# Attention with two mixture-of-experts layers on one core: other first loads, a row pass of one width, and VectorE work given to GpSimd

## The chip, the cores and the metric

The kernel runs on one core of a Trainium2 chip. The metric is the device time of one execution in microseconds. Before the change it is 1004.54 us, the median of three runs (1000.55 to 1005.47).

## What is computed

Block-causal attention feeds a top-2 mixture of experts, and that feeds a top-1 mixture of experts.

```
q, k, v: (4, 8, 576, 64)                     # batch, heads, sequence, head size
scores = q @ k.T / 8; masked where block_i < block_j (blocks of 64)
x = softmax(scores) @ v  ->  (2304, 512)     # heads side by side
logits = x @ w_gate + log1p(exp(x @ w_noise)) * noise      # 8 experts
for each row: the two best experts, softmax over the two
x = sum of weight * (relu(x @ w1[e]) @ w2[e])              # w1 512x1024, w2 1024x512
logits = x @ w_gate2 + modality_bias[modality]
out = softmax weight of the best expert * (relu(x @ m2w1[e]) @ m2w2[e])
```

All products are fp32 in quality: most are made of three products of high and low parts (`kh`/`kl`, `wh`/`wl`, `PTh`/`PTl`).

## The kernel before

The work runs in this order: 16 pairs of heads (4 batches of 4 pairs) in the attention, with the routing of finished batches beside it; then the experts of the first layer; then those of the second.

**A pair of heads** (`pair`, from L875) is cut into named steps. TK, TQ and T4 transpose k, q and their tails. KH, QH, A4 on ScalarE and KL, QL, D4 on VectorE make high and low parts. S0 to S8 are the scores, M the row maxima (`nm`, VectorE), E the exponentials (`p`, ScalarE, with row sums into `ss`). B transposes the exponentials, H and L split them into `PTh` and `PTl`. VX, V0, V1 are the products with v (`pa`), CX, C0, C1 copy them to `oT`.

**The row pass** (`xr`, L1074) is X0 and X1: for each head of the pair five products with `IW` (64 columns that turn `oT` into rows, and 16 columns of the gates) bring rows of 64 outputs and 16 gate logits into PSUM; four chunks have 128 rows, the last has 64 (L1078). XC0 and XC1 copy them to `xu`.

**R and R2** finish the softmax sums: GpSimd adds (R), VectorE takes four reciprocals of slices of `ss`, straight into `rr` (L1002, L1003). `out_rows` (L1090) multiplies `xu` by `rr` on GpSimd, into the rows `x` that are written to X1 in DRAM, and into `LH`, which holds the gate logits of all eight heads apart.

**Routing** (`route`, L650) runs three times, for batches 0 and 1 (behind pair 7), 2 (behind pair 11) and 3 (behind pair 15). It sums `LH` over heads by a reduction to `lg` (L659), picks the two best experts, counts places with products of `m`, and makes lists of rows per expert: `hot_b` (`sl_ob`) and `hot_a` (`sl_oa`, `sl_ov`) are one-hot arrays on VectorE, and `lists` multiplies them on TensorE, ten products for each batch. `early` (L1122) then turns part of the lists into indices (`si_u`, `ids`, `gp`, `idg`) and gathers the first rows of expert 0 and expert 1 from X1 into `wide` (`gather0`, L776).

**The first expert job** is planned with the attention (`first_steps`, L1162): JT, JH, JL bring its rows in, JM0 to JM7 are the eight hidden blocks (12 products each, `ps<-kh,wh`), JR and JV split them (`kp`), JS splits the next weights (`wl`). Its second matmul (`py`) and all later jobs follow in `run` (L1392), which transposes the gathered rows of the next job (`px`) between the halves of a second matmul.

**What sets the order.** TensorE, ScalarE and VectorE run what the loop from L1332 writes down: each step has a due time from a table (`SCHED`), the costs of L80 to L99 advance a clock for each engine, and the step that can start first, or is due first, is written next. GpSimd and SP get their instructions in the order in which that loop reaches them. An engine runs its list in order, so one late step holds what is written behind it.

**The start** (L1105 to L1113): nine matmuls on constant `ones`, then all loads of pair 0 to 2 on SP's queue, k and q of pair 0 first, then their tails, then v.

Of the kernel before, what the change touches and what calls it, by code (L numbers as in the profile page):

```python
# [30 lines left out]
def moe_kernel(tc, q, k, v, w_gate, w_noise, noise, w1, w2, mod_id, w_gate2, mod_bias, m2w1, m2w2, out):  # L31
# [72 lines left out]
    with ExitStack() as top:  # L104
# [9 lines left out]
        nc.scalar.preload_act_table_set("natural_log_exp_and_others")  # L114
# [167 lines left out]
        def hot_a(pool, a, n, a0, na, vals):  # L282

            oa = pool.tile([128, n, na], BF16, name="sl_oa")
            ov = pool.tile([128, n, NV, na], BF16, name="sl_ov")
            vec.tensor_tensor(oa, bc(lane[:, None, a0:a0 + na], [128, n, na]), bc(a[:, :, None], [128, n, na]), op=OP.is_equal)
            yield .8
            m = -(-n // 2) if n * na > 200 else n
            for c in range(0, n, m):
                s = slice(c, min(c + m, n))  # L290
                vec.tensor_tensor(ov[:, s], bc(oa[:, s, None, :], [128, s.stop - c, NV, na]),
                                  bc(vals[:, s, :, None], [128, s.stop - c, NV, na]), op=OP.mult)
                yield .3
            return ov
# [355 lines left out]
        def route(b0, nb):  # L650
# [6 lines left out]
            for b in range(b0, b0 + nb):  # L657
                c0 = 5 * (b - b0)
                vec.tensor_reduce(l[:, c0:c0 + 5], LH[:, b].rearrange("p c h e -> p c e h"), axis=AX, op=OP.add)  # L659
                yield .9  # L660
# [109 lines left out]
        LH = wide1[:, E * DM - B * 5 * H * 2 * E:].rearrange("p (b c h e) -> p b c h e", b=B, c=5, h=H)  # L770
# [33 lines left out]
        with ExitStack() as ph:  # L804
# [44 lines left out]
            def load(p, names):  # L849
# [7 lines left out]
                else:  # L857
                    r["t"] = ld.tile([128, 2, D], F32, name="tld")
                    tails = [(r["t"][64 * i:64 * i + 64], n) for i, n in enumerate("qk")]
# [3 lines left out]
                def ends():  # L863
                    for t, n in tails:
                        nc.sync.dma_start(t, src[n][b, 2 * hp:2 * hp + 2, 512:576, :].rearrange("h p d -> p h d"))
                if p:
                    ends()
                for n in names:
                    for i in range(2):
                        nc.sync.dma_start(r[n][:, 0:4, i, :],  # L870
# [4 lines left out]
            def pair(p):  # L875
# [214 lines left out]
                def out_rows():  # L1090
# [3 lines left out]
                    gps.tensor_tensor(LH[:, b, :, 2 * hp:2 * hp + 2].rearrange("p c h e -> p h c e"), xu[:, :, :, D:], rb(2 * E), op=OP.mult)  # L1094
# [11 lines left out]
            pw = ps_s.tile([128, 4, 128], F32, name="ps")  # L1106
            for _ in range(9):
                nc.tensor.matmul(pw, ones, bc(ones[:, None, :], [128, 4, 128]), start=True, stop=True)
            load(0, "kq")
            load(0, "v")  # L1110
            load(1, "kq")
# [155 lines left out]
            arrive = dict(zip(("TK", "TQ", "T4"), (4.2, 5.7, 6.8)))  # L1267
# [33 lines left out]
            def earliest(e, p, n):  # L1301
                t = clk[e] if p > 2 or n not in arrive else max(clk[e], arrive[n] + 5.5 * p)
# [390 lines left out]
```

## Time and profile before

| | |
|---|---|
| median of three runs | 1004.54 us (1000.55 to 1005.47) |
| profiled execution | 1002.42 us, span 1000.6 us |
| busy in the span: PE, DVE, ACT, POOL | 955.4, 723.9, 518.6, 492.9 us |
| chain that ended last | PE 72%, DVE 13%, issue 5%, ACT 3%, POOL 3%, DMA 2% |
| granted clock of TensorE, mean | 0.992 |

PE is TensorE's matmuls and PEld its weight loads, DVE is VectorE, ACT ScalarE, POOL GpSimd, SP SyncE. Nearly all instructions are recorded by one helper and so carry line L71: they are told apart by the tiles they write and read, as `ps<-kh,kp`. An fp32 matmul of the program is two weight loads and two matmuls in the trace. A row with "idle before" tells how long its engine stood idle and what ended that.

### The profile page before, as it was taken

To read this page: it belongs to the slowest core of one execution; us is meant where nothing else is said; L and a number is where in the kernel's file an instruction comes from. 1 tells how busy PE (TensorE), PEld (TensorE's weight loads), DVE (VectorE), ACT (ScalarE), POOL (GpSimd) and SP (SyncE) were. 2 spreads that over 40 slices of the span, in tenths; PEclk is the share of its full clock that TensorE was granted. 3 is DMA by queue.
4 is the path that set the end of the run, shared out by engine and by line. 5 is a ranking of instruction groups with operands and counts; after the bars stand their busy time and mean duration, and the time that the engine had idled before them with its cause. 6 is when DMAs were issued, how large, how long until landed. Compare 5 with 4: busy or idle time off the path is not lost.

```text
span 1000.6 us, 17459 instructions
## 1 busy us (share of the span) xinstructions
PE 955.4 (95%) x6058; PEld 863.6 (86%) x6058; DVE 723.9 (72%) x1761; ACT 518.6 (52%) x1156; POOL 492.9 (49%) x400
## 2 busy tenths in 40 slices
PE   7999998898999999999999999999999989999995
PEld 5988898787888997989899898989979879999994
DVE  5878879999968985568493957759788876455450
ACT  5989887778653253333333343333325445555551
POOL 6133141432221589768594857747476254333321
PEclk8999999999999999999999999999999999999998
DMA  5557743331067556555472745534366867776620
GB/s 126 103 156 229 208 122 82 77 82 50 26 202 254 95 138 187 131 138 115 107 147 75 161 105 127 123 80 64 110 149 178 288 215 241 225 223 216 209 84 13
DMA packets 158257, 141.59 MB, mean 142 GB/s; under 512 B 76233, under 2 KB 124745, under 8 KB 158034
## 3 DMA queue, kind: packets, MB, share of 16 engines
q1 hardware_dynamic: 140098, 107.18, 36.4%
q0 software_dynamic: 18064, 33.23, 16.5%
q8 instruction: 50, 0.82, 0.3%
q14 instruction: 45, 0.37, 0.1%
HBM read 112.54 MB, written 28.36 MB: 141 GB/s over the span
## 4 chain that ended last, share of the span: by engine, by line
PE 72%; DVE 13%; issue 5%; ACT 3%; POOL 3%; DMA 2%; SPq 1%; POOLq 0%; ACTq 0%
PE ph L71 28%; PE py L71 26%; PE pt L71 7%; PE ps L71 5%; PE pa L71 3%; PE px L71 2%; DVE nm L71 2%; DVE PTl L71 2%; DVE wl L71 2%; POOL wl L71 2%; ACT p L71 1%; DVE kp L71 1%; DMA xr<-X,ids 1%; ACT wh L71 1%; POOL LG L71 1%
## 5 line engine op out<-in xcount | busy, mean ns | idle before, releaser
L71 POOL TENSOR_TENSOR wl<-raw,wh 128x1024 fp32r<-128x1024 f32 x80 | 207.8, 2628 | 107.7 <-ACT wh L71 93.5
L71 PE MATMUL ph<-xth,wh 128*128 128x320 f32 (+2 forms) x800 | 240.9, 301 | 2.1 <-DVE kp L71 2.1
L71 PE MATMUL ph<-xth,wl 128*128 128x320 f32 (+2 forms) x800 | 239.7, 300 | 0.0
L71 PE MATMUL ph<-xtl,wh 128*128 128x320 f32 (+2 forms) x800 | 239.7, 300 | 0.0
L71 DVE SCALAR_TENSOR_TENSOR zero<-py,gts,wide 128x512 f32<-128x512 f32 x304 | 227.4, 748 | 8.3
L71 PE MATMUL py<-wh,kp 128*128 128x512 f32 x496 | 166.8, 396 | 0.0
L71 PEld LDWEIGHTS ph<-xth,wh 128*128 128x128 f32 x800 | 151.6, 189 | 3.7 <-DVE kp L71 2.9
L71 ACT ACTIVATE wh<-raw 128x1024 fp32r<-128x1024 f32 x144 | 150.9, 1053 | 2.8 <-DMA raw<-in_moe_w_dram 2.8
L71 PEld LDWEIGHTS ph<-xtl,wh 128*128 128x128 f32 x800 | 151.6, 190 | 0.7
L71 PEld LDWEIGHTS ph<-xth,wl 128*128 128x128 f32 x800 | 151.6, 189 | 0.0
L71 ACT ACTIVATE yr<-py,gts 128x512 f32<-128x512 f32 x60 | 41.4, 690 | 144.9 <-PE py L71 96.8
L71 PEld LDWEIGHTS py<-wh,kp 128*128 128x128 f32 x496 | 93.2, 188 | 18.3
L71 DVE SCALAR_TENSOR_TENSOR hl<-ph,hh 128x320 fp32r<-128x320 f32 (+2 forms) x100 | 46.3, 465 | 79.2 <-ACT hh L71 79.0
L71 PE MATMUL ps<-kh,kp 128*128 128x256 f32 (+5 forms) x320 | 98.4, 349 | 3.5 <-ACT p L71 1.5
L71 DVE TENSOR_TENSOR wl<-raw,wh 128x1024 fp32r<-128x1024 f32 x64 | 79.7, 1253 | 29.6 <-ACT wh L71 29.5
L71 PE MATMUL py<-wl,kp 128*128 128x512 f32 x248 | 96.7, 390 | 0.0
L71 POOL DMA_INDIRECT xr<-X,ids x55 | 58.7, 1066 | 72.9 <-PE px L71 44.2
L71 PE MATMUL py<-wh,hh 128*128 128x512 f32 x232 | 93.9, 405 | 0.0
L71 PE MATMUL py<-wl,hh 128*128 128x512 f32 x232 | 90.5, 390 | 1.7 <-POOL wl L71 1.7
L71 PE MATMUL py<-wh,hl 128*128 128x512 f32 x232 | 90.7, 391 | 0.0
L71 ACT ACTIVATE hh<-ph 128x320 fp32r<-128x320 f32 (+2 forms) x100 | 41.9, 418 | 93.6 <-PE ph L71 90.4
L71 DVE TENSOR_TENSOR xtl<-px,xth 128x512 fp32r<-128x512 f32 x58 | 40.0, 689 | 68.1 <-ACT xth L71 68.0
(249 smaller groups left out, 1822.0 us busy)
## 6 DMA issues: line engine op xcount, KB each, us to landing
raw<-in_moe_w_dram SPq DMA_DIRECT2D x144, 512.0 KB, 4.0
X<-zero SPq DMA_DIRECT2D x13, 512.0 KB, 4.3
kld<-in_k_dram SPq DMA_DIRECT2D x32, 128.0 KB, 2.8
qld<-in_q_dram SPq DMA_DIRECT2D x32, 128.0 KB, 2.9
vld<-in_v_dram SPq DMA_DIRECT2D x32, 128.0 KB, 2.7
X<-x SPq DMA_DIRECT2D x16, 256.0 KB, 2.4
wide<-in_moe_w_dram SPq DMA_DIRECT2D x4, 512.0 KB, 4.7
wide<-WG2T POOLq DMA_DIRECT2D x1, 2048.0 KB, 11.6
```

The costliest lines, as they stand in the source:

```text
L71: return f(*a, **kw)
```

## The change

It has seven parts.

- The loads of q of pair 0 are issued on ScalarE's queue, ahead of the loading of the activation table; on SP's queue k and q of pair 1 go ahead of v of pair 0.
- `spin` writes matmuls on `ones` wherever the loop sees a gap of more than 0.6 us on TensorE's clock in the first 60 us: 23 in all against 9.
- The last chunk of the row pass takes 128 columns of `oT` (rows 448 to 575); the copy takes the upper half.
- R2 is one reciprocal on VectorE (`ri`) and four copies on GpSimd that place it in `rr`.
- `LH` holds two sums: the first pair of a batch writes it, the others multiply in place and add, on GpSimd; the reduction to `lg` becomes one addition of two.
- In the first two routings the product `sl_ov` runs on GpSimd, in pieces of 3, 3, 3 and 1 of ten columns.
- The cost of an fp32 product and the arrival times of the first loads in the loop are other numbers.

```
-        return 2 * max(cols_of(i) * .00084, n * .00084) if dt == F32 else n * .000417 + .0145 * (clk["base"] is None)
+        return 2 * max(.09945, n * .00084) if dt == F32 else n * .000417 + .0145 * (clk["base"] is None)
...
-        def hot_a(pool, a, n, a0, na, vals):
+        def hot_a(pool, a, n, a0, na, vals, aside_=False):
...
+            eng = gps if aside_ else vec
...
-            m = -(-n // 2) if n * na > 200 else n
+            m = 3 if aside_ else -(-n // 2) if n * na > 200 else n
...
-                vec.tensor_tensor(ov[:, s], bc(oa[:, s, None, :], [128, s.stop - c, NV, na]),
+                eng.tensor_tensor(ov[:, s], bc(oa[:, s, None, :], [128, s.stop - c, NV, na]),
...
-                vec.tensor_reduce(l[:, c0:c0 + 5], LH[:, b].rearrange("p c h e -> p c e h"), axis=AX, op=OP.add)
+                vec.tensor_add(l[:, c0:c0 + 5], LH[:, b, :, 0], LH[:, b, :, 1])
...
-                ov = yield from hot_a(rt, a[:, n], 10, 0, NA1, va[:, n])
+                ov = yield from hot_a(rt, a[:, n], 10, 0, NA1, va[:, n], b0 + nb < B)
...
-                    ss = st["ss"]
+                    ri = sm.tile([128, 9], F32, name="ri")
+                    vec.reciprocal(ri, st["ss"][:, 0:9])
...
-                        vec.reciprocal(rr[0:64, h, :], ss[d, 0:9:2])
-                        vec.reciprocal(rr[64:128, h, 0:4], ss[d, 1:9:2])
+                        gps.tensor_copy(rr[0:64, h, :], ri[d, 0:9:2])
+                        gps.tensor_copy(rr[64:128, h, 0:4], ri[d, 1:9:2])
...
-                            n = 128 if c < 4 else 64
-                            ten.matmul(pt[0:n, c], st["oT"][:, h, 128 * c:128 * c + n], IW[:, 2 * hp + h], start=True, stop=True)
+                            c0 = 128 * c if c < 4 else S - 128
+                            ten.matmul(pt[:, c], st["oT"][:, h, c0:c0 + 128], IW[:, 2 * hp + h], start=True, stop=True)
...
-                        copy(xu[0:64, h, 4], pt[0:64, 4])
+                        copy(xu[0:64, h, 4], pt[64:128, 4])
...
-                    gps.tensor_tensor(LH[:, b, :, 2 * hp:2 * hp + 2].rearrange("p c h e -> p h c e"), xu[:, :, :, D:], rb(2 * E), op=OP.mult)
+                    lh = LH[:, b].rearrange("p c h e -> p h c e")
+                    part_ = xu[:, :, :, D:] if hp else lh
+                    gps.tensor_tensor(part_, xu[:, :, :, D:], rb(2 * E), op=OP.mult)
+                    if hp:
+                        gps.tensor_add(lh, lh, part_)
...
+            spin(8)
+            clk["pe"] = 4.2
+            load(0, "q", nc.scalar)
+            nc.scalar.preload_act_table_set("natural_log_exp_and_others")
+            load(0, "k")
+            load(1, "kq")
             load(0, "v")
-            load(1, "kq")
...
-            arrive = dict(zip(("TK", "TQ", "T4"), (4.2, 5.7, 6.8)))
+            arrive = dict(zip(("TK", "TQ", "T4"), ((4.7, 8.2, 15.2), (4.3, 9.2, 16.7), (5.8, 7.2, 17.8))))
...
+                if t < 60 and engine(n) == "pe" and t - clk["pe"] > .6:
+                    spin(int((t - clk["pe"] - .3) / .24))
```

The loop now writes another order for the attention. Behind the first expert job all five engines keep the order that they had, instruction by instruction.

TensorE at the start, before (`kld`, `qld` and `tld` are k, q and their tails as loaded, `ps<-kh,kp` scores):

```order
L71 MATMUL pt<-ident,kld 128x128 x4
L71 MATMUL pt<-ident,qld 128x128 x4
L71 MATMUL pt<-ident,tld 128x128
L71 MATMUL ps<-kh,kp_158 128x320
L71 MATMUL ps<-kl,kp_158 128x320
L71 MATMUL ps<-kh,kp_160 128x320
```

And in the change:

```order
L71 MATMUL pt<-ident,qld 128x128 x4
L71 MATMUL pt<-ident,kld 128x128 x4
L1117 LDWEIGHTS ones
L1117 MATMUL pt<-ones 128x512
L71 MATMUL pt<-ident,tld 128x128
```

```order
L1117 MATMUL pt<-ones 128x512
L71 MATMUL pt<-ident,kld 128x128 x4
L71 MATMUL ps<-kh,kp_157 128x320
L71 MATMUL ps<-kl,kp_157 128x320
L71 MATMUL ps<-kh,kp_159 128x320
```

The transposes of pair 0 are followed by eight matmuls on `ones`, and pair 1's k is transposed ahead of the first scores of pair 0.

TensorE at the end of the hidden blocks of the first expert (`ps<-kh,wl`), in the change; `pt<-sl_ov,sl_ob` is one of the ten list products of the second routing:

```order
L71 MATMUL ps<-kh,wh 128x256
L71 MATMUL ps<-kl,wh 128x256
L71 MATMUL ps<-kh,wl 128x256
L71 LDWEIGHTS sl_ob
L71 MATMUL pt<-sl_ov,sl_ob 128x200
```

Before, these ten stood ahead of the last transposes of the attention; now they stand behind all eight hidden blocks and directly ahead of `py`.

VectorE at the same place, before (`acc` adds the list products, and the rows to `idg` make the gather's indices of them):

```order
L71 TENSOR_TENSOR PTh<-pt,PTh 64x128
L71 TENSOR_TENSOR acc_99<-acc_99,pt 128x200
L71 TENSOR_SCALAR si_u_3854<-acc_99 128x3
L71 SCALAR_TENSOR_TENSOR si_t_3853<-acc_99,pad_76 128x3
L71 TENSOR_TENSOR PTl<-pt,PTh 128x512
```

And in the change:

```order
L71 TENSOR_TENSOR wl<-qld,wh 128x512
L71 SCALAR_TENSOR_TENSOR kp_4115<-ps,kp_4115 128x256
L71 TENSOR_TENSOR acc_98<-acc_98,pt 128x200
L71 TENSOR_SCALAR si_u_4142<-acc_98 128x3
L71 SCALAR_TENSOR_TENSOR si_t_4141<-acc_98,pad_75 128x3
L71 SCALAR_TENSOR_TENSOR si_u_4142<-si_u_4142,acc_98 128x3
L71 TENSOR_TENSOR ids_101<-si_t_4141,si_u_4142 128x3
```

```order
L71 TENSOR_SCALAR gp<-i_4139 128x3
L71 TENSOR_TENSOR idg_103<-gp,i_4139 128x3
L71 TENSOR_SCALAR base<-base 128x1
L71 TENSOR_TENSOR lg<-wide 128x80
```

The chain stood among the last subtractions of the attention; now it stands behind the last hidden block's subtraction (`kp`), and the third routing (`lg`) behind it.

## Rows read from the trace of the kernel before

**Rows 1.** Busy time by stage: start:end, length, each engine's busy us, PEclk, DMA share, GB/s.

```profile
0.00:30.00 30.00, 22.92 (x123) 18.64 (x124) 18.62 (x47) 18.09 (x54) 15.65 (x57) 0.89 0.57 122
30.00:150.00 120.00, 115.57 (x842) 106.47 (x842) 94.32 (x232) 105.83 (x328) 36.40 (x53) 1.00 0.61 166
150.00:280.00 130.00, 116.70 (x849) 105.61 (x848) 118.14 (x328) 94.81 (x298) 37.62 (x47) 0.99 0.26 67
280.00:340.00 60.00, 58.95 (x345) 52.30 (x344) 52.50 (x135) 24.37 (x44) 20.84 (x22) 1.00 0.73 212
```

**Rows 2.** What TensorE waited for, 0 to 30 us: us in total, times, longest.

```profile
PE pt L71 <- ACT p L71: 2.2, 1, 2.2
PE pt L71 <- DMA kld<-in_k_dram: 1.3, 1, 1.3
```

**Rows 3.** Busy time in one microsecond of the start.

```profile
22.00:23.00 1.00, 1.00 (x6) 1.00 (x5) 0.54 (x2) 0.67 (x2) 0.00 (x0) 0.50 0.94 210
```

**Rows 4.** TensorE in order of time, one call of the row pass: start, length, instruction.

```profile
93.68 1.01 PE L71 MATMUL pt<-IW,oT 128*128 128x80 f32 x8
...
94.62 0.13 PEld L71 LDWEIGHTS pt<-IW,oT 128*64 128x64 f32 x1
...
94.91 0.47 PE L71 MATMUL pa<-PTh,vs 128*128 128x448 f32 x1
```

**Rows 5.** What TensorE waited for, 150 to 280 us.

```profile
PE pt L71 <- DVE PTl L71: 5.1, 7, 1.6
PE pt L71 <- DVE PTh L71: 2.1, 2, 1.2
...
PE pt L71 <- DVE sl_a L71: 1.5, 1, 1.5
```

**Rows 6.** VectorE's groups, 0 to 290 us: xcount, busy us, mean ns, idle before.

```profile
L71 DVE TENSOR_TENSOR sl_ov<-sl_oa,vals 128x1000 bf16<-128x1000 bf16 x6 | 8.4, 1401 | 0.0
...
L71 DVE RECIPROCAL rr<-ss 64x5 f32<-64x5 f32 x32 | 5.7, 177 | 1.5 <-POOL ss L71 1.3
...
L71 DVE TENSOR_REDUCE lg<-wide 128x80 f32<-128x640 f32 x4 | 5.1, 1270 | 0.0
...
L71 DVE TENSOR_TENSOR ln<-ln,lg 128x80 f32<-128x80 f32 x1 | 0.2, 244 | 0.0
...
L71 DVE TENSOR_SCALAR sl_a<-pc 128x20 f32<-128x20 f32 x1 | 0.2, 159 | 0.0
```

**Rows 7.** GpSimd's groups, 0 to 290 us.

```profile
L71 POOL TENSOR_TENSOR x<-xu,rr 128x640 f32<-128x640 f32 x16 | 21.3, 1329 | 30.4 <-DMA tld<-in_q_dram 10.3 <-DVE nm L71 10.0 <-DVE kl L71 5.7
...
L71 POOL TENSOR_TENSOR wide<-xu,rr 128x160 f32<-128x160 f32 x16 | 9.3, 580 | 0.1
...
L71 POOL TENSOR_TENSOR ss<-ss 128x1 f32<-128x1 f32 x16 | 3.5, 219 | 85.9 <-ACT p L71 83.6 <-DMA qld<-in_q_dram 2.4
```

**Rows 8.** All engines in order of time, in the second routing.

```profile
247.22 1.25 POOL L71 TENSOR_TENSOR x<-xu,rr 128x640 f32<-128x640 f32 x1
247.23 1.27 DVE L71 TENSOR_SCALAR sl_a<-pc 128x10 f32<-128x10 f32 x1
...
248.88 0.66 PE L71 MATMUL pt<-ident,p 128*128 128x128 f32 x4 [0.95 <-DVE PTh L71]
```

**Rows 9.** VectorE and GpSimd in order of time, at the end of the hidden blocks.

```profile
268.43 0.36 DVE L71 TENSOR_TENSOR acc<-acc,pt 128x200 f32<-128x200 f32 x1
...
274.50 1.05 POOL L71 DMA_INDIRECT wide<-X,idg  x1 [0.78 <-PE ps L71]
...
291.30 0.36 DVE L71 SCALAR_TENSOR_TENSOR kp<-ps,kp 128x256 fp32r<-128x256 f32 x1
```

**Rows 10.** Landing of the three gathers by idg, from issue.

```profile
DMA to landing us min/median/max: 3.5/3.6/3.8
```

**Rows 11.** The chain that ended last, behind the hidden blocks: start, us, what.

```profile
288.42 2.74 PE py L71 x12
```

**Rows 12.** What TensorE waited for, 280 to 340 us.

```profile
PE pt L71 <- DVE m L71: 0.6, 1, 0.6
```

More of the change, by code (lines that the diff above doesn't have):

```diff
@@ L280, in hot_b @@
             return ob
-        def hot_a(pool, a, n, a0, na, vals):
+        def hot_a(pool, a, n, a0, na, vals, aside_=False):
             oa = pool.tile([128, n, na], BF16, name="sl_oa")
             ov = pool.tile([128, n, NV, na], BF16, name="sl_ov")
+            eng = gps if aside_ else vec
             vec.tensor_tensor(oa, bc(lane[:, None, a0:a0 + na], [128, n, na]), bc(a[:, :, None], [128, n, na]), op=OP.is_equal)
             yield .8
-            m = -(-n // 2) if n * na > 200 else n
+            m = 3 if aside_ else -(-n // 2) if n * na > 200 else n
             for c in range(0, n, m):
                 s = slice(c, min(c + m, n))
-                vec.tensor_tensor(ov[:, s], bc(oa[:, s, None, :], [128, s.stop - c, NV, na]),
+                eng.tensor_tensor(ov[:, s], bc(oa[:, s, None, :], [128, s.stop - c, NV, na]),
                                   bc(vals[:, s, :, None], [128, s.stop - c, NV, na]), op=OP.mult)
-                yield .3
+                yield ("pool", clk["pool"]) if aside_ else .3
             return ov
@@ L658, in route @@
                 c0 = 5 * (b - b0)
-                vec.tensor_reduce(l[:, c0:c0 + 5], LH[:, b].rearrange("p c h e -> p c e h"), axis=AX, op=OP.add)
-                yield .9
+                vec.tensor_add(l[:, c0:c0 + 5], LH[:, b, :, 0], LH[:, b, :, 1])
+                yield .3
             if b0 + nb == B:
@@ L769, in moe_kernel @@
         xs = wide1[:, 0:max(FIRST) * DM]
-        LH = wide1[:, E * DM - B * 5 * H * 2 * E:].rearrange("p (b c h e) -> p b c h e", b=B, c=5, h=H)
+        LH = wide1[:, E * DM - B * 5 * 4 * E:].rearrange("p (b c h e) -> p b c h e", b=B, c=5, h=2)
         rts = top.enter_context(ExitStack())
@@ L847, in copy, with load @@
                 act.activation(o, i, AF.Copy)
-            def load(p, names):
+            def load(p, names, eng=nc.sync):
                 b, hp = divmod(p, HP)
@@ L857, in load @@
                 else:
-                    r["t"] = ld.tile([128, 2, D], F32, name="tld")
-                    tails = [(r["t"][64 * i:64 * i + 64], n) for i, n in enumerate("qk")]
+                    tails = []
+                    if "k" in names:
+                        r["t"] = ld.tile([128, 2, D], F32, name="tld")
+                        tails = [(r["t"][64 * i:64 * i + 64], n) for i, n in enumerate("qk")]
                     for n in names:
@@ L864, in ends @@
                     for t, n in tails:
-                        nc.sync.dma_start(t, src[n][b, 2 * hp:2 * hp + 2, 512:576, :].rearrange("h p d -> p h d"))
+                        eng.dma_start(t, src[n][b, 2 * hp:2 * hp + 2, 512:576, :].rearrange("h p d -> p h d"))
                 if p:
@@ L869, in load @@
                     for i in range(2):
-                        nc.sync.dma_start(r[n][:, 0:4, i, :],
+                        eng.dma_start(r[n][:, 0:4, i, :],
                                           src[n][b, 2 * hp + i, 0:512, :].rearrange("(c p) d -> p c d", p=128))
@@ L1105, in moe_kernel, with spin @@
             nc.vector.memset(ones, 1.0)
[L1106 to L1109, printed above, removed]
+            pw = ps_r.tile([128, 4, 128], F32, name="pt")
+            def spin(n):
+                for _ in range(n):
+                    nc.tensor.matmul(pw, ones, bc(ones[:, None, :], [128, 4, 128]), start=True, stop=True)
+            spin(8)
[4 more added lines that the diff above has]
+            load(1, "kq")
             load(0, "v")
-            load(1, "kq")
             load(1, "v")
@@ L1301, in earliest @@
             def earliest(e, p, n):
-                t = clk[e] if p > 2 or n not in arrive else max(clk[e], arrive[n] + 5.5 * p)
+                t = clk[e] if p > 2 or n not in arrive else max(clk[e], arrive[n][p])
                 for d, k in before[n]:
```

1 line of the change is left out of this document (removed).

## The prediction, made before the change was run

> **What bounds the kernel now.** I read the busy times by stage first [rows 1]. The reader should see three things in them. From 280 us on TensorE is busy for 58.95 of 60 us, and the instruction order shows that every engine issues there what it issued before, so what the change does is done in the attention stage and at its end. Between 30 and 150 us TensorE is busy for 115.57 of 120 us with VectorE at 94.32: there only work taken off TensorE shortens the stage. Between 150 and 280 us, where the first two routings run beside the attention, VectorE is busy for 118.14 of 130 us and TensorE idles for 13.3. The list of what TensorE waited for in that stretch names VectorE, mostly the PTl subtractions that free a PSUM bank, and once a routing operation, sl_a [rows 5]. Between 0 and 30 us TensorE is idle for 7.1 us and its granted clock averages 0.89, that is 0.11 x 30 = 3.3 us of clock lost: the lower of its two levels, 1.2 GHz, stands in the single microseconds behind the early waits [rows 1 to 3].
>
> The profiled execution took 1002.42 us (span 1000.6 and 1.8 around it). It lies 2.1 under the median of the three runs, 1004.54. The sum is made against 1002.4.
>
> **The change part by part.**
>
> *Widened row pass.* One call of five products is ten pairs of a weight load and a matmul in the trace. It starts at 93.68 and the next product at 94.91, so it takes 1.23 us [rows 4]. Its first eight pairs, of full width, run from 93.68 for 1.01 us, the last 0.28 of it the length of the eighth matmul: seven steps in 0.73, 0.105 each. So the eighth starts at 94.41. The first load of 64 columns starts only at 94.62, twice a step later. With ten pairs of one width the next product would start three steps behind the eighth, at 94.41 + 3 x 0.11 = 94.74 instead of 94.91: 0.15 to 0.17 us less a call. There are 16 pairs x 2 heads = 32 calls: 4.8 us, nearly all on the path since TensorE bounds. Bounds 3 and 5; I take 4.5.
>
> *First loads.* q goes out on ScalarE's queue while k goes out on SP's, and pair 1's k and q are issued ahead of v. The wait of 1.3 us for kld goes; the fillers (14 more matmuls on the constant ones) are there to hold the clock through what is left. Scores of pair 0 still need both halves of q and k from ScalarE and VectorE, and the order puts pair 1's transposes ahead of them, so they start no earlier. From nothing, to all of 1.3 + 2.2 + 3.3 = 6.8 us [rows 1, 2]; a filler that overruns a gap that closed early costs a few tenths. The softmax chain on ScalarE, 2.2 us of wait, stays largely as it is; I take 3, bounds 1 and 5.
>
> *VectorE relief.* Removed in all: four reciprocals a pair, 64 in all, against one (two groups of 32 at 0.177, 11.3 us, down to about 16 x 0.18 = 2.9); six one-hot products of 1.40 = 8.4; four reductions of 1.27 against four additions of 0.24, so 4.1 [rows 6]. Sum 21 us, of which about 15.5 lie between 150 and 280: 8.4 + 3 x 1.03 + half the reciprocals. The most it can return there is the idle time, 13.3, and the clock that the stage lost, 0.01 x 130 = 1.3 [rows 1]. The least is 3: the waits for PTl and sl_a hang on more than the moved operations. VectorE falls from 91% to about 80% busy, which is where it stands between 30 and 150 us, and there TensorE idles 4%, about 5 us in 130. So I take 13.3 - 5 = 8. Between 30 and 150 us TensorE idles 4.4 us, part of it behind VectorE: I take 1.5, bounds 0 and 3.
>
> *GpSimd gains.* The products of 600 columns cost some 1.3 us each by the row of 640, three and a short one make 4.5 a batch; four copies of about 0.22 a pair; twelve additions of 0.58 [rows 7]. That is 3 x 4.5 + 16 x 0.88 + 7 = 35 us more on an engine busy for 89.7 of 280 [rows 1]. Its own queue has room. What GpSimd does to VectorE is another matter: while the row product x ran on GpSimd from 247.22 to 248.47, the ten-column sl_a on VectorE took 1.27, from 247.23 on, against 0.16 for one of twenty columns, and TensorE then waited 0.95 [rows 6, 8]. More GpSimd time between 150 and 280 means more such meetings; the price is inside the bounds of the relief, and is why I don't take all of 13.3. The Trainium skill (GPSIMD Engine Reference, sections 4.1 Engine selection and 8 Key points) says that an elementwise product belongs on VectorE, that GpSimd is about twice as slow with two inputs, and that the two share their SBUF interfaces. The trace agrees on the sharing [rows 8]; by the rule the relief would be given back in full and more, as in the third rival below (1012 us), by the row in part, as in the sum.
>
> *A wait that is new.* In the order, the ten list products of the second routing used to stand among the last attention products. Now they stand behind all eight hidden blocks of the first expert, directly ahead of its second matmul; on VectorE the addition that reads them stands behind the last hl subtraction. The chain from there: the last subtraction ended 291.66 where the hidden products ended about 288.4, so 3.2 us behind them; the addition 0.36 and nine tiny operations of 0.2, together 2.1; a gather needs 3.6 us to land [rows 9, 10]. So the gathered rows are there about 3.2 + 2.1 + 0.2 + 3.6 = 9 us behind the hidden products. TensorE has ten list products (1.1) and twelve py products, 2.74 [rows 11], before it wants them, 3.9 us. Before, they had landed long ago: the gather was issued at 274.50. New wait: about 4.5 to 5. Behind it on VectorE is queued the third routing, so the wait for m, 0.6 us today, grows by about 1 as well [rows 12]. I take +5.5. The least is 3 (if the subtraction is early), the most 9 (if the idle time also brings the clock down for a stretch, as behind the early waits, 1.7, and m is later still).
>
> **Sum:** -4.5 - 3 - 8 - 1.5 + 5.5 = -11.5, so 990.9 for an execution like the profiled one; a median may stand a little above, and I say 992. The ends of all terms together give -5 - 5 - 14.6 - 3 + 3 = -24.6 and -3 - 1 - 3 - 0 + 9 = +2.
>
> **The rivals.**
>
> *The end gives it back (0.17).* The new wait costs 8.5 with a fall of the clock, the relief returns 4, the loads 2, the steady stage 0.5: -4.5 - 2 - 4 - 0.5 + 8.5 = -2.5, so 1000. For it: waits of about 2 us have been followed by the low clock here [rows 2, 3]. Against: the row pass and the loads don't depend on it.
>
> *All of it arrives (0.18).* Stalls of the route stage vanish but for 2 us (-11), loads -4, row pass -5, steady stage -2, the wait at the end only 3: -19, so 983.5. For it: every long wait between 150 and 280 us names VectorE. Against: GpSimd's collisions.
>
> *VectorE is held by GpSimd, slower (0.10).* If each added GpSimd product keeps VectorE out while it runs, VectorE in the route stage has 118.1 - 15.5 + (13.5 + 7 x 1.46 = 23.7) = 126 us of work, and with the 9% that it idles today the stage takes 139 instead of 130: +9. Row pass -4.5, loads -2, end +7: +9.5, so 1012. The point from which it decides is 15.5 us of hold-ups added in that stage: under that VectorE is still relieved. For it: the hold-up shown, 1.1 us long beside one product [rows 8]. Against: GpSimd was busy 37.62 of 130 us in that stage already, and the held sl_a is 1.5 us of TensorE's waits there [rows 1, 5].
>
> *The loads and fillers do nothing* is inside the bounds of their term (1 instead of 3).
>
> **How the numbers follow.** Forecast 0.55, with a range of its own of 986 to 997; rivals 0.17, 0.18 and 0.10. The range of 8 in 10 takes in the forecast, most of the case at 983.5 and the case at 1000: 983 to 1002; left out are the slow rival and the tail below 983. A measurement can tell about 0.5%, 5 us, from no change. Faster by more than that is under 999.5: nearly all of the forecast, the good case and a third of the first rival, 0.75; within 0.5%: 0.16; slower: 0.09.
>
> **What would show it.** Right: the call of the row pass takes 1.08 us; the granted clock is 1.00 from about 5 to 30 us; between 150 us and the hidden products TensorE idles 5 to 7 us; TensorE's last hidden product comes some 15 to 17 us sooner; a wait of 4 to 5 us for a gather at the first px, which did not exist; and behind it everything shifted by one constant to the end. Wrong: reciprocals or reductions on VectorE that take over 1 us beside sl_ov on GpSimd, list products that wait for sl_ov behind the hidden blocks, or stages from 340 us on that change their own length by more than 2 us.

## The result, and the profile after

The change takes 992.8 us (median of 4 runs, 991.67 to 994.31) where the kernel before takes 1004.13 (4 runs). The ratio is 0.9892, with a 95% interval of 0.9867 to 0.9916: faster by 1.1%. The profiled execution took 991.67 us with a span of 989.9, 10.7 less in span than the one of before. I had said 992.0; the sum was -11.5.

Busy time by stage, after, for [rows 1] (start:end, length, PE, PEld, DVE, ACT, POOL, PEclk, DMA share, GB/s):

```profile
0.00:30.00 30.00, 26.80 (x158) 20.48 (x159) 21.71 (x53) 21.44 (x66) 16.32 (x61) 1.00 0.59 126
30.00:150.00 120.00, 117.64 (x873) 109.33 (x872) 93.94 (x226) 110.96 (x342) 45.98 (x93) 1.00 0.66 175
150.00:280.00 130.00, 115.26 (x882) 107.92 (x883) 103.98 (x292) 95.12 (x287) 58.73 (x95) 0.98 0.30 85
280.00:340.00 60.00, 59.09 (x339) 52.51 (x338) 54.42 (x146) 20.81 (x35) 21.91 (x22) 0.98 0.62 159
```

The first stage has its clock back (1.00 for 0.89) and 3.9 us more of TensorE's work (fillers among it), the second 2.1 more. In the third VectorE falls from 118.14 to 103.98 and GpSimd rises from 37.62 to 58.73, yet TensorE is not busier. The hidden products of the first expert now end at 268.26 us, 20.2 sooner than the 288.42 of before, and the stage holds what comes behind them.

What TensorE waited for after, 0 to 30 us (us in total, times, longest), for [rows 2]:

```profile
PE pt L1117 <- DVE ones L1112: 1.1, 1, 1.1
PE pt L71 <- DMA qld<-in_q_dram: 0.6, 1, 0.6
PE ps L71 <- DVE kl L71: 0.5, 1, 0.5
```

The same view, 150 to 280 us, for [rows 5]:

```profile
PE px L71 <- DMA wide<-X,idg: 6.7, 1, 6.7
PE pt L71 <- DVE PTl L71: 4.1, 6, 1.5
PE pt L71 <- DVE pc L71: 1.4, 1, 1.4
```

In the start the wait for kld and the 2.2 us behind the exponentials are gone. In the route stage PTl is still first, and a wait of 6.7 us for the gather that did not exist is now the longest of the kernel's first 340 us. One call of the row pass, for [rows 4], and groups of VectorE and GpSimd from 0 to 290 us, for [rows 6, 7]:

```profile
96.29 1.23 PE L71 MATMUL pt<-IW,oT 128*128 128x80 f32 x10
97.32 0.36 PE L71 MATMUL ps<-kh,kp 128*128 128x256 f32 x1
```

```profile
L71 DVE TENSOR_TENSOR sl_ob<-lane,sl_b 128x1280 bf16<-128x1280 f32 x3 | 5.5, 1847 | 1.9 <-PE pt L71 1.9
L71 DVE RECIPROCAL ri<-ss 128x9 f32<-128x9 f32 x16 | 3.3, 204 | 0.8 <-POOL ss L71 0.8
L71 DVE TENSOR_TENSOR lg<-wide 128x80 f32<-128x80 f32 x4 | 0.9, 229 | 0.0
...
L71 POOL TENSOR_TENSOR sl_ov<-sl_oa,vals 128x600 bf16<-128x600 bf16 x9 | 10.6, 1189 | 0.1
L71 POOL TENSOR_TENSOR wide<-wide,xu 128x160 f32<-128x160 f32 x12 | 6.9, 575 | 0.5
L71 POOL COPY rr<-ri 64x5 f32<-64x5 f32 x32 | 5.9, 184 | 46.6 <-DVE ri L71 45.6 <-DVE pos_k L71 0.3
...
L71 POOL TENSOR_TENSOR sl_ov<-sl_oa,vals 128x200 bf16<-128x200 bf16 x3 | 2.0, 669 | 0.0
```

A call takes 97.32 - 96.29 = 1.03 us for 1.23; all 32 calls, each from its start to the next product's, take 33.95 for 39.94. The three batches of sl_ov cost GpSimd 10.6 + 2.0 = 12.6 us where VectorE needed 8.4.

The ten list products of the second routing in the change's order of time, and the chain that ended last behind the attention, for [rows 9 to 11] (start, us, what):

```profile
268.10 1.03 PE L71 MATMUL pt<-sl_ov,sl_ob 128*128 128x200 bf16 x10
```

```profile
259.64 8.63 PE ps L71 x72
...
270.53 0.34 DVE kp L71
270.86 0.28 DVE acc L71
...
272.31 0.16 DVE idg L71
...
273.23 5.30 DMA wide<-X,idg
278.53 0.04 issue
278.58 1.11 PE px L71 x4
279.69 4.10 PE py L71 x12
...
288.32 0.21 DVE m L71
```

And the clock behind that wait (columns as above):

```profile
276.00:282.00 6.00, 3.42 (x10) 2.90 (x11) 1.31 (x2) 1.54 (x2) 0.79 (x1) 0.50 0.45 160
```

The reader sees the new wait as forecast: last subtraction, addition, small operations, gather, px. The gather starts 0.76 us behind the end of `idg` (272.47 to 273.23), as it did before (273.74 to 274.50). The granted clock is 1.00 up to it and at half, 1.2 GHz, while px and twelve py run, 4.1 us for the 2.74 of [rows 11]. The first product of the next expert (ph) starts at 290.90 for 301.64 before, 10.7 sooner; the last one 11.0 sooner. So nothing of the gain is made or lost behind 291 us, and of the 19.7 us by which the first hidden product comes sooner (253.1 for 272.8) the end has taken back 9.0.

### The profile page after: what moved, and what is told of

Same layout as the page of the kernel before. It is cut to its first block, busy times and chain, and to the rows that moved or that the text cites. A ratio compares the mean times of both kernels' runs of the same rounds, so it can differ in the third digit from the quotient of the medians.

```text
span 989.9 us, 17527 instructions
## 1 busy us (share of the span) xinstructions
PE 949.4 (96%) x6072; PEld 860.7 (87%) x6072; DVE 703.6 (71%) x1707; ACT 520.9 (53%) x1156; POOL 521.0 (53%) x488
## 4 chain that ended last, share of the span: by engine, by line
PE 73%; DVE 9%; issue 5%; ACT 5%; DMA 4%; POOL 3%; SPq 1%; POOLq 0%; ACTq 0%; DVEq 0%
PE ph L71 28%; PE py L71 27%; PE pt L71 7%; PE ps L71 6%; PE pa L71 3%; PE px L71 2%; DVE wl L71 2%; ACT p L71 2%; POOL wl L71 2%; ACT kp L71 1%; DVE kp L71 1%; DMA xr<-X,ids 1%; DVE nm L71 1%; DVE PTl L71 1%; DMA qld<-in_q_dram 1%
## 5 line engine op out<-in xcount | busy, mean ns | idle before, releaser
L71 POOL TENSOR_TENSOR wl<-raw,wh 128x1024 fp32r<-128x1024 f32 x80 | 207.5, 2623 | 106.4 <-ACT wh L71 92.2
L71 PE MATMUL ph<-xth,wh 128*128 128x320 f32 (+2 forms) x800 | 241.2, 302 | 2.1 <-DVE kp L71 2.1
L71 PE MATMUL ph<-xth,wl 128*128 128x320 f32 (+2 forms) x800 | 240.0, 300 | 0.0
L71 PE MATMUL ph<-xtl,wh 128*128 128x320 f32 (+2 forms) x800 | 240.0, 300 | 0.0
L71 DVE SCALAR_TENSOR_TENSOR zero<-py,gts,wide 128x512 f32<-128x512 f32 x304 | 227.5, 748 | 8.3
L71 PE MATMUL py<-wh,kp 128*128 128x512 f32 x496 | 168.1, 399 | 0.0
L71 PEld LDWEIGHTS ph<-xth,wh 128*128 128x128 f32 x800 | 151.7, 190 | 4.0 <-DVE kp L71 2.8
L71 PEld LDWEIGHTS ph<-xtl,wh 128*128 128x128 f32 x800 | 151.7, 190 | 0.7
L71 PEld LDWEIGHTS ph<-xth,wl 128*128 128x128 f32 x800 | 151.7, 190 | 0.0
L71 ACT ACTIVATE wh<-raw 128x1024 fp32r<-128x1024 f32 x144 | 150.8, 1053 | 0.6 <-DMA raw<-in_moe_w_dram 0.5
L71 ACT ACTIVATE yr<-py,gts 128x512 f32<-128x512 f32 x60 | 41.3, 689 | 147.1 <-PE py L71 104.6
L71 PEld LDWEIGHTS py<-wh,kp 128*128 128x128 f32 x496 | 94.0, 189 | 18.5
L71 DVE SCALAR_TENSOR_TENSOR hl<-ph,hh 128x320 fp32r<-128x320 f32 (+2 forms) x100 | 46.4, 465 | 79.1 <-ACT hh L71 78.9
L71 DVE TENSOR_TENSOR wl<-raw,wh 128x1024 fp32r<-128x1024 f32 x64 | 80.1, 1259 | 29.8 <-ACT wh L71 29.1
L71 PE MATMUL py<-wl,kp 128*128 128x512 f32 x248 | 97.4, 393 | 0.0
L71 PE MATMUL ps<-kh,kp 128*128 128x256 f32 (+5 forms) x320 | 95.7, 340 | 0.6 <-ACT p L71 0.4
L71 POOL DMA_INDIRECT xr<-X,ids x55 | 57.5, 1045 | 73.5 <-PE px L71 44.2
L71 PE MATMUL py<-wh,hh 128*128 128x512 f32 x232 | 94.0, 405 | 0.0
L71 DVE TENSOR_TENSOR xtl<-px,xth 128x512 fp32r<-128x512 f32 x58 | 40.0, 690 | 74.3 <-ACT xth L71 74.3
L71 PE MATMUL py<-wl,hh 128*128 128x512 f32 x232 | 90.6, 390 | 1.7 <-POOL wl L71 1.7
L71 ACT ACTIVATE hh<-ph 128x320 fp32r<-128x320 f32 (+2 forms) x100 | 41.8, 418 | 95.1 <-PE ph L71 91.6
L71 PE MATMUL py<-wh,hl 128*128 128x512 f32 x232 | 90.9, 392 | 0.0
```

The costliest lines, as they stand in the source:

```text
L71: return f(*a, **kw)
```

## The experiments

Twelve kernels, five to twelve executions each. Each ratio is against the kernel before in executions beside it, whose median lay between 1001.34 and 1004.13 us; so kernels are compared by ratio or by starts, and a difference of two times can be off by some 3 us. The table has the starts (us) of four products of TensorE in the profiled executions: the first hidden product, py, px, and ph. The first tells what the attention took, the rest what its end took.

| kernel | us, ratio (95%) | hidden | py | px | ph |
|---|---|---|---|---|---|
| before | 1004.13 | 272.8 | 288.3 | 291.0 | 301.6 |
| the change | 992.8, 0.9892 (0.9867 to 0.9916) | 253.1 | 268.9 | 278.6 | 290.9 |
| second product on VectorE | 985.16, 0.9819 (0.9795 to 0.9843) | 253.1 | 268.9 | 271.6 | 283.0 |
| clock held | 990.95, 0.9871 (0.9850 to 0.9892) | 253.2 | 269.1 | 278.9 | 290.3 |
| narrow row pass | 998.23, 0.9945 (0.9926 to 0.9965) | 257.4 | 273.5 | 282.6 | 294.5 |
| GpSimd part undone | 994.13, 0.9902 (0.9877 to 0.9928) | 262.7 | 277.8 | 280.5 | 291.2 |
| start undone | 997.7, 0.9957 (0.9941 to 0.9974) | 258.3 | 274.0 | 283.4 | 295.5 |
| old loads, no fillers | 995.73, 0.9936 (0.9922 to 0.9950) | 256.7 | 272.4 | 281.7 | 294.2 |
| row pass alone, on before | 1007.27, 1.0051 (1.0036 to 1.0065) | 277.4 | 292.5 | 295.3 | 305.9 |
| the same, order kept | 999.56, 0.9978 (0.9962 to 0.9993) | 268.2 | 283.3 | 286.0 | 296.7 |
| second product and reciprocals on VectorE | 990.15, 0.9882 (0.9862 to 0.9901) | 257.9 | 273.7 | 276.7 | 287.8 |
| lists not held | 993.9, 0.9927 (0.9902 to 0.9951) | 262.3 | 277.2 | 280.0 | 290.9 |
| lists held 2 us | 989.37, 0.9878 (0.9855 to 0.9901) | 253.3 | 272.5 | 275.2 | 286.1 |
| both products on VectorE | 994.3, 0.9930 (0.9906 to 0.9953) | 259.7 | 278.5 | 281.2 | 292.1 |

### The wait at the end: the place of the lists

```
-                ov = yield from hot_a(rt, a[:, n], 10, 0, NA1, va[:, n], b0 + nb < B)
+                ov = yield from hot_a(rt, a[:, n], 10, 0, NA1, va[:, n], b0 == 0)
```

> The changed kernel with one edit: in the second routing the one-hot product sl_ov runs on VectorE again (two pieces of about 1.4 us), in the first it stays on GpSimd. In the order the ten list products then stand a third of the way into the hidden blocks instead of behind them. Theory A (the place of the lists made the new wait): the gather is issued some 8 us before the hidden products end, the wait of 6.67 us in front of px is under 0.5, the clock stays at 1.00 there (6.8 us at half speed, worth about 3, go as well), VectorE's added 2.8 us costs TensorE at most 2: 992 - 6.7 - 3 + 1.5 = about 984. Rival B (the gather is late because weight loads share the queues, wherever the lists stand): a wait of 3 or more stays, 990 or above. Rival C (the product on VectorE costs as much in waits for PTl as it gives): hidden products start 5 us later or more, 988 to 992.

985.16 us: theory A, and the best kernel of this study. The attention is as long as in the change (253.1), the two pieces back on VectorE cost nothing there, and the gather's wait is gone. What is left of TensorE's waits from 260 to 330 us, all of it on VectorE:

```profile
PE ph L71 <- DVE kp L71: 1.2, 2, 0.9
PE px L71 <- DVE xtl L71: 1.0, 1, 1.0
PE pt L71 <- DVE m L71: 0.2, 1, 0.2
```

GpSimd in order of time in the same kernel:

```profile
266.83 1.06 POOL L71 DMA_INDIRECT wide<-X,idg  x1 [3.83 <-DVE lg L71]
```

The gather is issued at 266.83, 4.8 us ahead of px, where the change issues it at 273.23. That is 2.2 us ahead of the end of the hidden products (269.07), not the 8 expected, and still enough. ph comes 7.9 us sooner than in the change: that is what the place of ten small products cost. In the two kernels of the section on the loop's clock of GpSimd the lists stand earlier with the product left on GpSimd, and there the wait for the gather is gone as well; so it is the place of the lists, not the engine of the product.

### The wait at the end: the clock

```
+                            if nx is j10 and left[0] == 0:
+                                pw = ps_r.tile([128, 4, 128], F32, name="pt")
+                                for _ in range(26):
+                                    nc.tensor.matmul(pw, ones, bc(ones[:, None, :], [128, 4, 128]), start=True, stop=True)
                             nx.cols(left[0])
```

> The changed kernel with 26 matmuls on the constant ones written between the twelve py products and px, so that TensorE is busy through the new wait. Theory A (the idle time itself brought the clock down): granted clock 1.00 from 275 to 283, the twelve py behind px take about 2.75 us instead of 4.3 and px half, so 991.7 - 2.5 to 3 = about 989 if the fillers end before the rows land. Rival (the clock does not hang on this wait, or the fillers overrun the landing): same time or up to 1.5 slower.

The clock part of theory A came, as the window shows (for the one of the change above, 0.50); the time did not:

```profile
276.00:282.00 6.00, 4.77 (x24) 3.22 (x23) 1.42 (x2) 1.55 (x2) 0.93 (x1) 1.00 0.47 161
```

px takes 0.67 us for 1.11 and the twelve py behind it 2.8 for 4.1, 1.7 us in all, but ph starts at 290.35, only 0.55 sooner; 990.95 us can't be told from 992.8. Two things took the rest. The rows land 0.34 us later here (278.87 for 278.53). And the wait for m grew from 0.5 to 1.1: between px and m stand VectorE's subtractions and weight splits (xtl, wl) and the third routing, and m comes 8.9 us after the landing for 9.8. So about half of what the clock gives back, 0.9 us from landing to ph, arrives; the other half was hidden behind VectorE.

### The lists and the loop's clock of GpSimd

```
-                yield ("pool", clk["pool"]) if aside_ else .3
+                yield ("pool", clk["pool"]) if aside_ and c + m >= n and False else .3
```

> The changed kernel, products of both routings on GpSimd as in the change, but the planning loop no longer holds a routing back until its own clock for GpSimd has passed (each piece of sl_ov counts as 0.3 us). The list products of the second routing then stand ahead of all hidden blocks. Theory A (it was the loop's clock of GpSimd that put the lists behind the hidden blocks, not GpSimd itself): the wait in front of px is gone; on TensorE the lists now wait for sl_ov, whose four pieces take about 4.4 us from 3 us behind sl_ob, so 1 to 3 us of wait at each of three places: 992 - 8 + 2 to 6 = 986 to 990. Rival B (GpSimd is quick enough and the lists don't wait): 983 to 985, better than the product on VectorE. Rival C (the lists wait long and the clock falls): 991 or more.

```
-                yield ("pool", clk["pool"]) if aside_ else .3
+                yield 2.0 if aside_ else .3
```

> As the run before it, with each piece of sl_ov counted as 2.0 us times 0.7 in the loop instead of 0.3: list products of the second routing stand a sixth of the way into the hidden blocks. Theory A: no wait in front of px (the gather is issued some 10 us before it), lists no longer waiting for sl_ov by more than 0.5 each: 982 to 985, the same as the product on VectorE or a little better, as VectorE is 2.8 us lighter. Rival (new order stalls elsewhere in the first routing): 987 to 990.

Without the hold the wait in front of px is gone, as theory A said, but TensorE waits for GpSimd's product instead (its waits from 130 to 330 us):

```profile
PE pt L71 <- DVE PTl L71: 5.1, 7, 1.6
PE pt L71 <- POOL sl_ov L71: 4.5, 6, 1.8
```

The hidden products start 9.2 us later and the time is 993.9, in rival C's range, though without its fall of the clock. With 2 us a piece they start where the change has them and ph comes 4.8 sooner, but 989.37 is the rival's time: the last row pass (258.1) now stands between the hidden blocks, and py starts 3.5 later. So the loop's clock of GpSimd did put the lists where they are. Without any hold TensorE waits for GpSimd; with a short one the attention is as quick as in the change; and of the ways tried for the second routing the product on VectorE is the quickest (ph at 283.0, against 286.1 to 290.9).

### What the GpSimd part is worth

> The changed kernel with the GpSimd part undone: reciprocals, sums of gate logits and both one-hot products back on VectorE; first loads, fillers, row pass and planner costs stay as changed. The list products then stand ahead of the hidden blocks again. Theory A (what the GpSimd part gains in the attention, about 10 us, the wait at the end takes back): hidden blocks start about 263 instead of 253, no wait in front of px, time 990 to 994, no different from the change. Rival B (the relief is most of the gain even after the end): 996 or more. Rival C (the GpSimd part hurts on balance): under 988.

The edit puts back the four reciprocals, the eight separate sums in `LH` with the reduction to `lg`, and the call of `hot_a`, as the lines with - in the diff of the change have them. 994.13 us: theory A. From 150 us to the first hidden product, this kernel and then the change (columns as before):

```profile
150.00:262.70 112.70, 99.25 (x751) 90.90 (x749) 108.26 (x304) 87.14 (x268) 33.69 (x43) 1.00 0.22 58
```

```profile
150.00:253.10 103.10, 95.03 (x730) 88.76 (x731) 90.28 (x260) 84.93 (x262) 45.59 (x83) 1.00 0.24 63
```

VectorE has 18 us less to do in the change, and the attention ends 9.6 us sooner; at ph the two kernels are 0.3 us apart. Of the 9.6 us, 5.4 are idle time of TensorE (103.10 - 95.03 = 8.1 against 112.70 - 99.25 = 13.5), and about 1.0 is that the ten list products stand behind the hidden blocks in the change and ahead of them here; the rest is busy time whose cause the runs don't show. Nor is the idle time shown to be VectorE's relief alone, since the order differs too: the kernel without the hold has VectorE nearly as light (94.65 us busy from 150 us to its first hidden product) and TensorE idles 14.3 us there. As the change stands, moving work to GpSimd buys nothing that these runs can tell; with the second routing's product back on VectorE it buys 9.0 us (994.13 to 985.16).

```
-                    ri = sm.tile([128, 9], F32, name="ri")
-                    vec.reciprocal(ri, st["ss"][:, 0:9])
+                    ss = st["ss"]
...
-                        gps.tensor_copy(rr[0:64, h, :], ri[d, 0:9:2])
+                        vec.reciprocal(rr[0:64, h, :], ss[d, 0:9:2])
```

> The kernel with the second routing's product on VectorE (985.2), and the four reciprocals a pair back on VectorE, straight into rr, without copies on GpSimd. Theory A (the reciprocals are the small part of the relief: 8 us of VectorE's time, half of it in the stretch where VectorE binds): hidden products 2 to 4 us later, 987 to 989. Rival B (the copies on GpSimd delay rr and xu, or hold VectorE, as much as the reciprocals cost): 984 to 986. Rival C (the reciprocals are most of the relief): 991 or more.

Against the 985.16 kernel the reciprocals cost 4.8 us by the starts of the hidden products and of ph (6.3 by the ratios): between theory A's 2 to 4 and rival C. 1.0 of it is there at the first row pass (37.09 for 36.08). All engines in order of time show where much of the rest went:

```profile
231.14 3.34 DVE L71 SCALAR_TENSOR_TENSOR ex<-u,ex 128x40 f32<-128x40 f32 x1
...
231.67 1.26 POOL L71 TENSOR_TENSOR x<-xu,rr 128x640 f32<-128x640 f32 x1
...
232.89 1.53 POOL L71 TENSOR_TENSOR vs<-vld,vs 128x640 fp32r<-128x640 f32 x1
...
235.23 0.66 PE L71 MATMUL pt<-ident,p 128*128 128x128 f32 x2 [3.16 <-DVE PTl L71]
```

A forty-column operation of VectorE, 0.2 us elsewhere, lasts until GpSimd's two products of 640 columns are done (234.48 and 234.42), and TensorE idles 3.16 us behind it. How far the 4.8 us are the reciprocals and how far this one meeting, the run doesn't separate.

```
-                ov = yield from hot_a(rt, a[:, n], 10, 0, NA1, va[:, n], b0 + nb < B)
+                ov = yield from hot_a(rt, a[:, n], 10, 0, NA1, va[:, n], False)
```

> The changed kernel with the one-hot products of both routings back on VectorE; reciprocals' copies and sums of gate logits stay on GpSimd. The lists of the second routing stand just ahead of the hidden blocks. Theory A (the reciprocals, worth 5 us, and the sums carry the relief; a product on GpSimd in the first routing is worth 1 to 3): no wait in front of px, 985 to 988. Rival B (first routing's product is most of what is left of the relief): 989 or more. Rival C (GpSimd's products are worth nothing): 984 or less.

994.3 us: rival B. The first routing's product on VectorE too, and the hidden products start 6.6 us later than with it on GpSimd, and ph 9.1 later, since the last row pass now stands behind the first hidden products. So in the first routing the product is worth more on GpSimd than I gave it; but the order is another one, and the granted clock averages 0.97 from 150 us to the hidden products for 1.00, so the run doesn't give the product's own worth. With both products on VectorE the copies and sums on GpSimd buy nothing (994.3 against 994.13 with the whole part undone); the pieces of the GpSimd part don't add up one by one.

### The row pass

```
-                            c0 = 128 * c if c < 4 else S - 128
-                            ten.matmul(pt[:, c], st["oT"][:, h, c0:c0 + 128], IW[:, 2 * hp + h], start=True, stop=True)
+                            n = 128 if c < 4 else 64
+                            ten.matmul(pt[0:n, c], st["oT"][:, h, 128 * c:128 * c + n], IW[:, 2 * hp + h], start=True, stop=True)
```

> The changed kernel with the last chunk of the row pass 64 columns wide again; the planned order is the same, instruction by instruction. Theory A (row pass on the path everywhere): a call takes 1.23 us again, 32 calls cost 6.0 us more in sum, the time rises by 5 to 6: 997 to 998. Rival (beside the first routings it hides under VectorE's waits): the calls are longer but the time rises by 3 at most, 995 or less.

998.23 us, near theory A in time. By the starts, the hidden products come 4.3 later and ph 3.6, between theory A and the rival; the profiled execution loses another 3.4 us in a stretch far behind the edits (last section), so the time's nearness to theory A is partly chance. And the row pass is not on the path everywhere. From 36 to 126 us, narrow first, then the change:

```profile
36.00:126.00 90.00, 89.18 (x652) 82.12 (x651) 70.61 (x167) 81.32 (x253) 33.88 (x68) 1.00 0.70 191
```

```profile
36.00:126.00 90.00, 87.76 (x650) 81.22 (x649) 70.37 (x167) 82.89 (x253) 33.80 (x67) 1.00 0.71 192
```

TensorE is busier by 1.4 us with the narrow form and gets exactly as far: from the first call of pair 0 to that of pair 6 it is 89.7 us narrow and 90.0 wide. Twelve shorter calls bring nothing there; TensorE only idles more. What sets the pace there the runs don't show (ScalarE, the next busiest, is busy for 82.89 of the 90 us). All 4.3 us come behind 126 us, beside the routings: the other way round than I had it.

> The kernel before with the widened row pass alone; the loop plans anew with its old costs. Theory A (the row pass pays where TensorE is the limit and not where another engine paces it): 32 calls shorter by 0.19, 6.0 in sum, of which 3 to 4.5 arrive: ratio 0.9955 to 0.997. Rival (beside the routings VectorE at 91% busy binds, so that nothing arrives there): under 2, ratio 0.998 or more. Second rival (all of it): 0.994.

> The kernel before with the widened row pass and the changed kernel's cost of an fp32 product in the loop, so that the loop plans the order of before nearly row by row. Theory A (row pass alone was slower by 0.5% only because the loop, which counts a product of 128 columns dearer, planned another order for the routings): with the order kept a gain of 2.5 to 4.5, ratio 0.9955 to 0.9975. Rival (the wider products cost something themselves, or free TensorE only to wait on VectorE): ratio 0.999 or more.

The first of these has the wide form of the diff on the kernel before, the second also the changed line of the cost (`max(.09945, n * .00084)`). Alone, the row pass makes the kernel slower by 0.5%, which no theory held: the old cost counts a product of 128 columns dearer, the loop writes another order, and TensorE idles 127.4 - 110.21 = 17.2 us between 150 us and the hidden products at a mean clock of 0.96, where the kernel before idles 122.80 - 109.50 = 13.3 at 0.99:

```profile
150.00:277.40 127.40, 110.21 (x785) 99.78 (x784) 118.61 (x320) 91.64 (x288) 31.74 (x43) 0.96 0.23 60
```

With the order of before nearly kept, the hidden products start 4.6 us sooner than before, 0.9 of it won ahead of the first call, and ph 4.9; in time the ratio is 0.9978, a little less of a gain than theory A gave; in the profiled executions 2.3 us are lost again in the stretch far behind the edits. So the number in the cost table is as much a part of the change as the wider product.

### The start

Two kernels. The first takes the loads and the fillers back to those of before and leaves the arrival times, so that the order stays (its diff is below); the second takes the arrival times back too, and has nine matmuls on `ones` for eight:

```
-                if t < 60 and engine(n) == "pe" and t - clk["pe"] > .6:
+                if t < 0 and engine(n) == "pe" and t - clk["pe"] > .6:
...
-            load(0, "q", nc.scalar)
...
-            load(0, "k")
-            load(1, "kq")
+            load(0, "kq")
             load(0, "v")
+            load(1, "kq")
```

> The changed kernel with the old sequence of loads on SP's queue and no fillers (eight matmuls on ones at the start), the planned order of the attention as in the change, instruction by instruction. Theory A (loads and fillers act by the clock and the first waits alone): half speed for two stretches before 30 us and a wait of about 1.3 for a load: first row pass 3 to 4 us later, the pace from there stays 14.8 a pair: 995.5 to 996.5. Rival (the new order needs its loads early: pair 1's k is transposed ahead of pair 0's scores, so the old sequence stalls TensorE longer than before): first row pass 5 us later or more, 998 or above.

> The changed kernel with its whole start undone: all first loads on SP's queue in the old sequence, nine matmuls on ones and no fillers, the old arrival times in the planning loop. Row pass and GpSimd part stay. Theory A (start worth what its clock and waits show, 3 to 4 us, and the quicker pace from 36 to 126 us, 14.8 us a pair instead of 15.5, comes with the order that the loop then writes): clock back at half speed for two stretches before 30 us, first row pass about 40 instead of 36, pace 15.5 again, 3 + 3 to 4 = 998 to 1000. Rival B (the pace comes from elsewhere, the cost of the fp32 product in the loop): pace stays 14.8, time 996. Rival C (the start is given back at the first routing): 993 to 994.

The first, 995.73 us, is theory A in time, and its first row pass comes 3.5 us later (39.59 for 36.09), as theory A had it; the second, 997.7, lies between theory A and rival B. By the ratios they are 0.4% and 0.65% behind the change, by ph 3.3 and 4.6 us. With old loads in the new order TensorE waits for pair 1's k as the rival had it, 4.7 us and not 1.3, and the clock falls again (waits from 0 to 36 us; window from 0 to 30):

```profile
PE pt L71 <- DMA kld<-in_k_dram: 4.7, 1, 4.7
```

```profile
0.00:30.00 30.00, 22.11 (x119) 17.90 (x120) 18.63 (x45) 17.95 (x56) 15.68 (x58) 0.89 0.56 119
```

In the first kernel the hidden products start 3.6 us later. How much of that is the loads and how much the fillers, no run separates. From the first call of pair 0 to that of pair 6 it takes 90.0 us still (15.0 a pair); with the old arrival times 91.5, and 93.0 in the kernel before. So the quicker steady stage belongs to the order that the loop writes, about half of it to the arrival times; it is there with the GpSimd part undone (89.9) and with the narrow row pass (89.7).

## Why the prediction was right

The time (992.8 for 992.0), the new wait with its place and cause, and the signs of the large terms were right. That the time came within 1 us is partly luck: the gain at the hidden products is 19.7 us where the terms ahead of the wait gave 17.0, the wait took 9.0 where its term gave 5.5, and the two misses nearly cancel. The terms, as undoing one part at a time shows them at the first hidden product: row pass 4.3, loads and fillers 3.6, arrival times 258.3 - 256.7 = 1.6, GpSimd part 9.6, together 19.1 of the 19.7 that the change is ahead there (272.8 - 253.1). The end takes back 19.7 - 10.7 = 9.0. About 1.0 us stands in both, for the ten list products, which only changed sides.

- **Row pass, -4.5 said, 4.3 measured, by a working that was wrong twice, so the close number is luck.** A call is shorter by 0.19 and not by 0.15, 6.0 in sum. And "nearly all on the path since TensorE bounds" failed: where TensorE was busiest, nothing arrived, since something else sets the pace there; beside the routings, nearly all did.
- **First loads, -3 said, 3.6 measured.** The clock is 1.00 in the whole stage, as said; the part of the loads and that of the fillers are not told apart.
- **VectorE relief from 30 to 150 us, -1.5 said.** About 3 us came between 36 and 126 us, but not from relief: they stay with the GpSimd part undone.
- **VectorE relief from 150 to 280 us, -8 said, 9.6 measured.** TensorE idles 103.1 - 95.03 = 8.1 us in the stage, a little over the 5 to 7 named: 5.4 less than with the GpSimd part undone, where the term wanted 8. The rest of the 9.6 is the moved list products and busy time, and the relief of VectorE is not separated from the other order. The last hidden product comes 20.2 sooner, not 15 to 17.
- **The wait that is new, +5.5 said, 9.0 measured**, at the top of its bounds of 3 to 9 (7.9 by the kernel with the second product on VectorE). This term was mis-sized. The chain had four parts: last subtraction behind the products (3.2 said, 2.6 measured from 268.26 to 270.86), small operations (2.1, now 1.6), issue (0.2, now 0.76, which the trace of before shows as well), landing (3.6, now 5.3 beside weight loads, at a DMA share of 0.91 from 272 to 279.5 us against 0.56 from 274.5 to 281 for the gathers of before). I took the landing from a quieter stretch. That the loads are what slows it is argued from the shares; no run takes them away. TensorE idles 6.67 us where I said 4.5 to 5; the fall of the clock, which I kept for the upper bound, came too, and is worth 0.55 us at ph by the run that holds it, 0.9 from the landing on. The wait for m did not grow (0.5 for 0.6).

**The rivals.** "The end gives it back" had the wait almost right (8.5 with the clock's fall) but its small relief was wrong. "All of it arrives" had the relief nearly right and the end wrong; the kernel without the wait at the end takes 985.16 for its 983.5. Its reason, that every long wait between 150 and 280 us names VectorE, was misread: the same view of before has `PE pt L71 <- ACT p L71: 1.7, 1, 1.7`, ScalarE's. "VectorE is held by GpSimd" fell. Of VectorE's rows between 0 and 300 us, those over 0.5 us longer than the shortest of their operation and shape are 7 before, 6.9 us too long in sum, and 6 after, 6.3 us. The added work on GpSimd brought no more meetings of this kind. The Trainium skill (GPSIMD Engine Reference, section 8 Key points) says that GpSimd contends for the shared interfaces with VectorE instructions that read two SBUF inputs or run in a two-port mode. The trace agrees in part: all 6 held rows after have two inputs in SBUF, as has the 3.34 us one above, but 3 of the 7 before read one (two of them are `sl_a`, 1.27 and 1.17 us), and whether those run in a two-port mode no run shows. One of the 6, and GpSimd's row beside it, which end at 233.15 and 233.09:

```profile
231.52 1.57 POOL L71 TENSOR_TENSOR vs<-vld,vs 128x640 fp32r<-128x640 f32 x1
231.75 1.40 DVE L71 TENSOR_TENSOR ln<-ln,nz 128x40 f32<-128x40 f32 x1
```

By the same section of the Trainium skill an elementwise product is about twice as slow on GpSimd; here it was 12.6 us for 8.4, 1.5 times. In the first routing the kernel with the product on GpSimd was still the faster one (985.16 for 994.3), with the other order that goes with it.

## What to carry to other kernels

When work goes to a slower but idle engine, look at who reads the result and what stands behind that reader: ten products that slid behind a block of 15 us cost 8 us, and putting one of three batches back recovered them. A faster instruction on the engine with the highest busy share pays only where that engine sets the pace (12 shorter calls of the row pass moved nothing between 36 and 126 us, with TensorE 99% busy); check it by a stretch's progress, not by its busy time. Where a cost table writes the order, an edit to the work and an edit to the table have to be tried apart, since either can outweigh the other.

## What the runs showed of the hardware that was not expected

- A VectorE operation of 0.2 us can last through several GpSimd operations in a row: 3.34 us, until 234.48, where GpSimd's second product ended at 234.42.
- The same gather of rows took 3.5 to 3.8 us to land before, and 5.3 for the first and 4.0 for the quickest beside weight loads after.
- Half speed over px and twelve py, 5.2 us for 3.5, cost 0.9 us at the next stage: the rest was hidden behind VectorE's chain.
- One stretch behind the edits, of some 126 us (from about 700 us on, between the 1400th and the 1800th ph product), took 125.6 us in the profiled execution of the change and 129.1 in the one with the reciprocals back, with no edit there (the other executions lie between); why is not known. The rest of the expert stages repeats within about 1 us. That is why the table compares starts, and why a time can move by 2 us more than its attention did (998.23 for the narrow row pass, 5.4 more than the change, whose ph is only 3.6 later).
